# Pairing two lone token tiles across batches, and a re-sorted instruction order, in a fused attention and Fourier mixing kernel

## The chip, the cores and the metric

The kernel runs on one core of a Trainium2 chip. Its engines work side by side and meet only through semaphores: TensorE (PE, with PEld for the loading of weights), VectorE (DVE), ScalarE (ACT), GpSimd (POOL) and SyncE (SP, which only issues DMAs here). The metric is the device time of one execution in microseconds; lower is better.

## The reference

Cosine attention over 8 batches, 12 heads, 448 tokens and 64 features per head, then a Fourier mix and a two-layer network with a residual:

```python
q_n = q / (norm(q) + 1e-06); k_n = k / (norm(k) + 1e-06)
attn = softmax(q_n @ k_n.T / tau)                  # tau = 0.1
x = (attn @ v).transpose(0, 2, 1, 3).reshape(8, 448, 768)
u = x + real(fft(fft(x, axis=1), axis=2))
un = (u - mean(u)) / sqrt(var(u) + 1e-06)
out = u + relu(un @ w_ch1) @ w_ch2                 # 768 -> 3072 -> 768
```

## The kernel before

Python code records every operation of all batches, and a scheduler, the function schedule of class Plan, then lays them out on the five engines. It keeps a clock for each engine, takes durations from a table (TIMES) and times of transfers from another (FLOW), and gives a free engine the ready operation of the lowest priority number. The priority is that of the stage (10 + 100 b for the attention of batch b, 5000 + b for the products of the network, which so fill whatever PE time is left) plus a correction from the table SHIFT, by the operation's name and its count. Only the order goes into the program; each engine then works through its list, and an instruction waits on semaphores for what it reads. So the order of the list is what the scheduler decides, and what a late transfer costs is decided on the chip. The table LATE adds a margin, in microseconds, behind a transfer or a POOL operation on which an operation depends: the scheduler plans its user that much later.

A batch goes through these steps. norm(b) loads q and k, sums squares, scales them (POOL, L896) and transposes them by DMA (SP, L902). attn(b) goes through six pairs of heads. It forms scores by key tile (L973; the last 64 keys by L986), ACT takes the exponential (L951), and PE multiplies by v (L1004, L1010). The scores of one step are written as a group: before the change batches 4 to 7 score three key tiles in a group, batches 1 to 3 two, in groups that run across two head pairs. fft(b) does the Fourier sums on PE (L1134, L1138 over tokens; L1188 and L1191, the last transform, over features, named fd). DVE adds and subtracts them (L1222) and adds them to x (L1233, giving the tiles U and their sums), then normalises each tile to F (L1282, named un). SP transposes it into one of four columns of UNT (L1303, named tru).

A batch has 448 tokens, but works on token tiles of 128: since the transform pairs token t with 448 - t, an even batch has three tiles, and an odd batch four, two of them half filled by an even batch. The network runs over units of one or two such tiles. An up product (L1350) multiplies 128 columns of w_ch1 with a unit: 144 matmuls of 128 columns for a lone tile, 144 of 256 columns for a pair. For a pair the down product (L1494) uses seven products of 12 matmuls (names m1 to m7) instead of eight, with sums of hidden rows formed on DVE (L1593, named s1 to s4) and sums of weights formed once (TX). A lone tile takes four products of 12 (y0 to y3). Some results go through ACT (L1514) and a POOL addition (L1519), the others straight from PSUM on DVE (L1530). Two output tiles, OUTB, collect the result; one kind of tile is stored by SP, the others are scattered by POOL (L1552). The pair of batch 6 and both pairs of batch 7 also save up products in that way (function ups, L1445).

The function units says which tiles go together. Before the change a unit lies within a batch:

```python
for n in (1, 2) if b in (0, self.nb - 2) else (2, 2) if b % 2 else (2, 1):
    sl += [2 * (u % 2) + x for x in range(n)]
```

So batches 0, 2, 4 and 6 have one lone tile each: the first of 0 and 6, the third of 2 and 4. ffn(b) runs the units of batch b, and all products of the network stand in one chain on PE. Where the finished plan leaves a gap on PE in a stretch of little PE work, the function fill puts warm matmuls there (L1737 on W1b), which compute nothing that is used.

Of the kernel before, what the change touches and what calls it, by code (L numbers as in the profile page):

```python
# [13 lines left out]
DM = H * DH  # L14
# [11 lines left out]
TF = 4  # L26
ORDER = (0, 1, 2, 3, 5, 4)
# [456 lines left out]
def t_dve(n, mode=1):  # L484
    return 0.1 + n / (960.0 * mode)
# [15 lines left out]
class Kern:  # L501
# [405 lines left out]
    def attn(self, b):  # L907
# [31 lines left out]
        for pos, j in enumerate(ORDER):  # L939
# [18 lines left out]
            if b < 1:  # L958
                steps = [[(pos, kt)] for kt in range(3)]
            elif b >= 4:  # L960
                steps = [[(pos, kt) for kt in range(3)]]
            else:
                steps = [[(pos, 0), (pos, 1)], [(pos, 2), (pos + 1, 0)]] if pos % 2 == 0 else [[(pos, 1), (pos, 2)]]
# [834 lines left out]
```

## Time and profile before

| | |
|---|---|
| runs | 577.16 us median of 3 (577.0 to 578.32) |
| profiled execution | span 575.2 us from the first to the last instruction; the median of the runs is 1.96 us longer |
| PE busy | 555.8 us, 97% of the span |
| DVE, ACT, POOL busy | 430.6, 385.3, 220.3 us |
| granted TensorE clock | 0.999 of full speed |

Busy times of PE are modelled: a matmul counts from its issue to its end, and successive ones overlap. How fast PE works through a list is read better from the chain of waits, where a piece ends when the next begins. Rows of the trace give start and length in microseconds, engine, line, operation and tiles, and in brackets the idle time before, with what ended it.

### The profile page before, as it was taken

To read this page: it belongs to the slowest core of one execution; us is meant where nothing else is said; L and a number is where in the kernel's file an instruction comes from. 1 tells how busy PE (TensorE), PEld (TensorE's weight loads), DVE (VectorE), ACT (ScalarE), POOL (GpSimd) and SP (SyncE) were. 2 spreads that over 40 slices of the span, in tenths; PEclk is the share of its full clock that TensorE was granted. 3 is DMA by queue.
4 is the path that set the end of the run, shared out by engine and by line. 5 is a ranking of instruction groups with operands and counts; after the bars stand their busy time and mean duration, and the time that the engine had idled before them with its cause. 6 is when DMAs were issued, how large, how long until landed. Compare 5 with 4: busy or idle time off the path is not lost.

```text
span 575.2 us, 16313 instructions
## 1 busy us (share of the span) xinstructions
PE 555.8 (97%) x6766; PEld 436.2 (76%) x6766; DVE 430.6 (75%) x917; ACT 385.3 (67%) x724; POOL 220.3 (38%) x332
## 2 busy tenths in 40 slices
PE   3899999999999999999999999999999999989997
PEld 3569787676787686878788787778778787959694
DVE  8989968996669869975669669776778579986262
ACT  7898885564876885687558875577637853747270
POOL 7534414356329544612370724523270210041303
PEclk9999999999999999999999999999999999999999
DMA  9999999975459739952595429743591210023001
GB/s 188 224 233 171 166 186 130 171 152 111 111 94 103 178 76 135 142 127 62 112 121 93 102 80 147 150 84 85 89 113 29 43 57 28 2 43 72 28 28 56
DMA packets 187898, 62.20 MB, mean 108 GB/s; under 512 B 166800, under 2 KB 185616, under 8 KB 187824
## 3 DMA queue, kind: packets, MB, share of 16 engines
q1 hardware_dynamic: 129856, 38.35, 33.7%
q0 software_dynamic: 57968, 22.81, 30.9%
q8 instruction: 53, 0.87, 0.6%
q14 instruction: 21, 0.17, 0.1%
HBM read 51.90 MB, written 11.01 MB: 109 GB/s over the span
## 4 chain that ended last, share of the span: by engine, by line
PE 60%; DVE 4%; ACT 2%; issue 0%; DVEq 0%; ACTq 0%
PE PS L1494 23%; PE PS L1350 20%; PE PS L1445 6%; PE PS L1010 4%; PE PS L973 3%; DVE U L1233 1%; PE PS L1004 1%; PE PS L986 1%; ACT E L951 1%; DVE ACG L1222 1%; ACT F L1275 1%; PE PS L1134 1%; PE PS L1191 1%; DVE SM L885 1%; DVE HQ L1593 1%
## 5 line engine op out<-in xcount | busy, mean ns | idle before, releaser
L1350 PE MATMUL PS<-UNT,W1b 128*128 128x256 bf16 (+1 forms) x1872 | 186.1, 256 | 1.2 <-DMA UNT<-F 0.6
L1350 PEld LDWEIGHTS PS<-UNT,W1b 128*128 128x128 bf16 x1872 | 155.5, 98 | 20.1 <-issue 2.7
L951 ACT ACTIVATE E<-PS 128x900 bf16<-128x900 f32 (+1 forms) x192 | 148.0, 827 | 19.1 <-PE PS L973 16.6
L1494 PE MATMUL PS<-W2b,HQ 128*128 128x384 bf16 x768 | 133.1, 326 | 0.0
L896 POOL TENSOR_TENSOR QH<-STG,SM 128x256 bf16<-128x256 f32 x126 | 82.3, 679 | 91.9 <-DVE SM L702 73.3
L1494 PEld LDWEIGHTS PS<-W2b,HQ 128*128 128x128 bf16 x768 | 73.3, 98 | 46.2 <-issue 0.7
L1519 POOL TENSOR_TENSOR OUTB<-OUTB,U 128x192 f32<-128x192 f32 x66 | 43.2, 675 | 138.5 <-ACT OUTB L1514 137.3
L1366 ACT ACTIVATE HQ<-PS 128x512 bf16<-128x512 f32 x81 | 48.2, 595 | 40.0 <-PE PS L1350 39.5
L1494 PE MATMUL PS<-TX,HQ 128*128 128x384 bf16 (+2 forms) x408 | 69.7, 321 | 1.8 <-ACT MV L1278 1.6
L883 ACT ACTIVATE QH<-STG 128x384 f32<-128x384 f32 x84 | 42.7, 520 | 25.8 <-DVE SM L885 21.3
L1494 PEld LDWEIGHTS PS<-TX,HQ 128*128 128x128 bf16 x408 | 38.4, 98 | 25.7 <-ACT MV L1278 2.0
L1593 DVE TENSOR_TENSOR HQ<-HQ 128x1536 bf16<-128x1536 bf16 (+1 forms) x69 | 49.5, 721 | 9.9 <-ACT HQ L1366 7.1
L885 DVE TENSOR_REDUCE SM<-QH 128x6 f32<-128x384 f32 x84 | 44.7, 544 | 11.3 <-ACT QH L883 11.0
L1010 PE MATMUL PS<-VB,E 128*128 128x65 bf16 x1152 | 51.4, 193 | 0.0
L1366 DVE TENSOR_SCALAR HQ<-PS 128x512 bf16<-128x512 f32 x45 | 31.0, 688 | 23.8 <-PE PS L1350 23.4
L1010 PEld LDWEIGHTS PS<-VB,E 128*128 128x128 bf16 x1152 | 47.7, 97 | 1.2
L1552 POOL DMA_INDIRECT out_dram<-OUTB,IDX x21 | 23.8, 1134 | 56.9 <-DVE OUTB L1530 51.7
L1004 PE MATMUL PS<-VZ,E 128*128 128x130 bf16 x192 | 41.6, 219 | 0.5 <-ACT E L951 0.2
L973 PE MATMUL PS<-QK 64*128 64x225 bf16 (+2 forms) x864 | 39.6, 227 | 0.1
L1233 DVE SCALAR_TENSOR_TENSOR U<-ACG,X 128x768 bf16<-128x768 f32 (+4 forms) x39 | 39.1, 1015 | 0.8
L1530 DVE TENSOR_TENSOR OUTB<-PS,OUTB 128x384 f32<-128x384 f32 x33 | 18.2, 553 | 25.7 <-PE PS L1494 21.9
L1514 ACT ACTIVATE OUTB<-PS 128x384 f32<-128x384 f32 x33 | 16.1, 488 | 29.5 <-PE PS L1494 29.1
(191 smaller groups left out, 793.6 us busy)
## 6 DMA issues: line engine op xcount, KB each, us to landing
STG<-in_q_dram SPq DMA_DIRECT2D x18, 384.0 KB, 4.0
STG<-in_k_dram SPq DMA_DIRECT2D x18, 384.0 KB, 3.8
VB<-in_v_dram POOLq DMA_DIRECT2D x24, 192.0 KB, 7.1
W1b<-in_moe_w_ch_dram POOLq DMA_DIRECT2D x12, 384.0 KB, 7.7
W2b<-in_moe_w_ch_dram POOLq DMA_DIRECT2D x12, 384.0 KB, 7.2
out_dram<-OUTB SPq DMA_DIRECT2D x7, 384.0 KB, 3.4
W2b<-in_q_dram SPq DMA_DIRECT2D x2, 576.0 KB, 10.0
W2b<-in_k_dram SPq DMA_DIRECT2D x2, 576.0 KB, 10.7
```

The lines of the kernel that those rows point to most:

```text
L885: P.add("dve", lambda v, o=SS[:, i, H // ns * x:H // ns * (x + 1)], sq=sq: v.tensor_reduce(o, sq.rearrange("p (h d) -> p h d", d=DH), AX.X ...
L896: r = v.tensor_tensor(v3(qh)[:, h:h + 4], v3(buf)[:, h:h + 4], RN[:, i, h:h + 4].unsqueeze(2).to_broadcast((128, 4, DH)), AluOp.mult)
L951: return a.activation(o, self.PS[:, bk:bk + nc_, 0:SQ2], ACTF.Exp, scale=1.0 / self.tau)
L973: i = pe.matmul(self.PS[:, bk + h, c0:c0 + n], self.KT[r, jj, kt * 128:(kt + 1) * 128], self.QT[r, jj, cols], start=True, stop=True)
L1004: r = pe.matmul(o, st(6), self.VZ[:, j, :], start=not split, stop=(split and i == 0), skip_group_check=True)
L1010: r = pe.matmul(o[:, 65 * h:65 * h + 65], st(2 * kt + h), self.VB[:, kt, 2 * j + h, :], start=(split and i == h == kt == 0), stop=((not sp ...
L1233: self.snu.append(P.add("dve", lambda v: v.scalar_tensor_tensor(two(U[o0:o0 + n, ut, :]), src, 1.0, two(X[i0:i0 + n, x, :]), AluOp.mult, A ...
L1350: r = pe.matmul(self.PS[:, bk, x * n:(x + 1) * n], self.W1b[:, j, ft * 128:(ft + 1) * 128], self.UNT[:, j, cs], start=(j == 0), stop=(j == ...
L1366: return e.activation(o, i, ACTF.Relu) if e is self.nc.scalar else e.tensor_relu(o, i)
L1494: r = pe.matmul(self.PS[:, bk, 0:n], lhs(f), rhs(f), start=(start and f == 0), stop=(stop and f == NF // 2 - 1), skip_group_check=True)
L1519: r = g.tensor_tensor(self.OUTB[:, ob, xs], self.OUTB[:, ob, xs], self.U[:, ut, xs], AluOp.add)
L1593: P.add("dve", lambda v: v.tensor_tensor(cs(o), cs(a), cs(bq), op), 0.16 + 0.3 * len(ks), -0.5, f"{nm}{ks[0]}_{b}", reads=rd, writes=[x fo ...
```

## The change

Units now run on across batches: all tiles of all batches stand in one list, and two neighbours make a pair except the first tile of batch 0 and the third of batch 2. The third tile of batch 4 is paired with the first of batch 5, and the fourth of batch 5 with the first of batch 6; that tile of batch 5 is normalised later, by the new function unheld, into a buffer of the q and k tiles (QH). A unit runs in ffn of its last batch. Batch 3 scores three key tiles per group, as batches 4 to 7 do, so with 12 matmuls in six groups instead of 8 in nine. The first scores of a batch are ordered behind the last transform of the batch before. LATE is larger for the squares, the copy of key tails (ktd) and of a query column (qdup), and SHIFT has new entries for nearly every operation from batch 1 on. Line numbers grow with the table; L1350 becomes L1714, L1494 L1858, L973 L1317, L1233 L1577, L1282 L1629, L1593 L1958.

```diff
+ONES = ((0, 0), (2, 2))
+HELD = (5, 3)
...
-LATE = {r"W[12]_\d+": 1.5, "tmd": 2.0, r"sq\d_\d": 1.5, r"sq[KQT]\d_1": 1.5, r"ktd\d": 2.0, r"qdup\d": 2.0, r"qk\d._[2-7]": 1.5, ...
+LATE = {r"sq6_[2-7]": 4.0, r"W[12]_\d+": 1.5, "tmd": 2.0, r"sq\d_\d": 2.0, r"sq[KQT]\d_1": 1.5, r"ktd\d": 3.5, r"qdup\d": 4.0, r"qk\d._[2-7]": 1.5, ...
...
+    "fd0_1": {0: -141.9791}, "qe0_1": {0: -36.7192}, "pq0_1": {0: -257.8814, 1: 714.6408}, "u0_1": {0: -254.5074, 1: 210.4266},
...
-            elif b >= 4:
+            elif b >= 3:
                 steps = [[(pos, kt) for kt in range(3)]]
...
-                      tiles=new, acquire=new, margin=0.3, order=([self.last_qk] if self.last_qk else []) + self.pvs[-2:-1])
+                      tiles=new, acquire=new, margin=0.3, order=([self.last_qk] if self.last_qk else []) + self.pvs[-2:-1] + (self.fd_ops[-1:] if b and pos == 0 else []))
...
+            if (b, ui) == HELD:
+                self.held = (ut, rn, lp, slot, col)
+                continue
...
+    def unheld(self):
+        P = self.P
+        ut, rn, lp, slot, col = self.held
+        b, ui = HELD
+        r = self.qh_next % 6
+        self.qh_next += 1
+        qn = [f"QH{r}"] + ["QH1x"] * (r == 1) + ["QH4x"] * (r in (3, 4))
+        P.add("dve", lambda v: v.tensor_scalar(self.QH[:, r, :], self.U[:, ut, 0:DM], self.MV[:, ut, 0:1], self.RS[:, ut:ut + 1], AluOp.add, AluOp.mult),
+              t_dve(DM, 4) + 0.16, lp, f"un{ui}_{b}", reads=rn + [f"MV{ut}", f"RS{ut}"], writes=qn)
+        self.last_tru = P.add("sp", lambda sy, sem: sy.dma_start_transpose(self.UNT[:, :, col:col + 128], self.QH[:, r, :]).then_inc(sem, 16),
...
     def units(self):
+        self.slots = [[0] * len(self.tiles(b)) for b in range(self.nb)]
+        order = [(b, i) for b in range(self.nb) for i in range(len(self.tiles(b)))]
+        u = x = 0
+        self.pairs = []
+        while x < len(order):
+            n = 1 if order[x] in ONES else 2
+            for y in range(n):
+                b, i = order[x + y]
+                self.slots[b][i] = 2 * (u % 2) + y
+            self.pairs.append(order[x:x + n])
+            u, x = u + 1, x + n
...
-        for i, two in ((0, 0), (1, 1)) if b == self.nb - 2 else [(i, i + 1 < len(tiles)) for i in range(0, len(tiles), 2)]:
+        for k, unit in enumerate([u for u in self.pairs if u[-1][0] == b]):
+            two = len(unit) == 2
...
-                    self.up(b, (i, i + 1), chunks, True)
+                    self.up(b, unit, chunks, True)
+                    if unit[1][0] == HELD[0] and unit[0][0] < b:
+                        self.unheld()
```

What the new order does is seen at three joins, on one or two engines each.

PE behind the last transform of batch 5 (L1188, L1191), before the change. The lone tile of batch 4 follows the last down products of the pair before it:

```order
L1188 MATMUL PS<-CS,E 128x96
L1191 MATMUL PS<-CS,E 128x2x96
L1494 MATMUL PS<-W2b,HQ 128x384 x20
L1494 MATMUL PS<-TX,HQ 128x384 x12
L1350 MATMUL PS<-UNT,W1b 128x128 x72
L973 MATMUL PS<-QK 128x128 x2
```

The same place in the change (L1532, L1535 are the transform, L1317 the scores of batch 6):

```order
L1532 MATMUL PS<-CS,E 128x96
L1535 MATMUL PS<-CS,E 128x2x96
L1858 MATMUL PS<-W2b,HQ 128x384 x16
L1858 MATMUL PS<-TX,HQ 128x384 x24
L1858 MATMUL PS<-W2b,HQ 128x384 x16
L1317 MATMUL PS<-QK 128x128 x2
```

Behind it come that group of 24 scores, 12 more down matmuls with the four matmuls of the key tail among them, a second group of 24, and then the joined unit of batches 4 and 5 (L1714, 256 columns). The up product that stood 32 down matmuls behind the transform now stands 76 and two groups behind it.

DVE between the second half of that transform and the first normalised tile, before the change (L1233 adds to U, L1270 the mean, L1282 normalises; L1366 and L885 are evacuations and sums of squares):

```order
L1233 SCALAR_TENSOR_TENSOR U,ACG<-ACG,X 32x768
L1366 TENSOR_SCALAR HQ<-PS 128x512
L1233 SCALAR_TENSOR_TENSOR U,MV<-ACG,X 1x768
L1270 TENSOR_SCALAR MV<-ACG 128x1
L1270 TENSOR_SCALAR MV<-MV 128x1
L885 TENSOR_REDUCE SM<-QH 128x6 x2
L1366 TENSOR_SCALAR HQ<-PS 128x512
L885 TENSOR_REDUCE SM<-QH 128x6
L1366 TENSOR_SCALAR HQ<-PS 128x512
L1282 TENSOR_SCALAR F<-U,MV 128x768
```

And in the change (L1566 subtracts and adds the halves, L1895 adds a product into OUTB, L1577 adds to U, L1629 normalises):

```order
L1566 TENSOR_TENSOR ACG<-PS,ACG 128x388 x2
L1895 TENSOR_TENSOR OUTB<-PS,OUTB 128x384
L1577 SCALAR_TENSOR_TENSOR U,ACG<-ACG,X 97x768
L1629 TENSOR_SCALAR F<-U,MV 128x768
L1229 TENSOR_REDUCE SM<-QH 128x6
L1577 SCALAR_TENSOR_TENSOR U,MV<-ACG,X 64x768
```

The first tile of batch 5 is normalised behind the first addition of the second half, no longer behind all four and their means.

PE in front of the first unit of batch 2, before the change (L973 and L986 are the first scores of batch 3, L1004 and L1010 its products with v; three more such pairs follow, and then L1350 with the unit):

```order
L1494 MATMUL PS<-TX,HQ 128x384 x24
L1494 MATMUL PS<-W2b,HQ 128x384 x8
L973 MATMUL PS<-QK 128x225 x8
L1494 MATMUL PS<-W2b,HQ 128x384 x16
L973 MATMUL PS<-QK 128x225 x8
L1494 MATMUL PS<-TX,HQ 128x384 x4
L986 MATMUL PS<-QK,KTD 128x225 x2
L1494 MATMUL PS<-TX,HQ 128x384 x8
L1004 MATMUL PS<-VZ,E 128x130
L1010 MATMUL PS<-VB,E 128x65 x6
```

And in the change, where L2107 are the warm matmuls:

```order
L1858 MATMUL PS<-TX,HQ 128x384 x24
L1858 MATMUL PS<-W2b,HQ 128x384 x24
L1858 MATMUL PS<-TX,HQ 128x384 x12
L1317 MATMUL PS<-QK 128x225 x12
L2107 MATMUL PS<-W1b 128x128 x18
L1330 MATMUL PS<-QK,KTD 128x225 x2
L1714 MATMUL PS<-UNT,W1b 128x256 x18
```

The products with v that stood in front of the unit are behind it, and 18 warm matmuls have come in.

DVE at the end of batch 6, before the change (L1593 is a comb pass of the network, the second of the two with 1536 columns being s2; L1253 copies, L1465 keeps hidden rows):

```order
L1222 TENSOR_TENSOR ACG<-PS,ACG 128x388 x2
L1593 TENSOR_TENSOR HQ<-HQ 128x512
L1465 TENSOR_TENSOR HQ<-PS,E 128x384
L1233 SCALAR_TENSOR_TENSOR U,ACG<-ACG,X 97x768
L1593 TENSOR_TENSOR HQ<-HQ 128x512
L1253 COPY ACG<-ACG 1x2
L1253 COPY U<-U 1x768
L1593 TENSOR_TENSOR HQ<-HQ 128x1536
L1270 TENSOR_SCALAR MV<-ACG 128x1
L1593 TENSOR_TENSOR HQ<-HQ 128x1536
```

And in the change:

```order
L1566 TENSOR_TENSOR ACG<-PS,ACG 128x388
L1829 TENSOR_TENSOR HQ<-PS,E 128x384 x2
L1831 TENSOR_SCALAR HQ<-HQ 128x384
L1958 TENSOR_TENSOR HQ<-HQ 128x512 x2
L1958 TENSOR_TENSOR HQ<-HQ 128x1536
L1629 TENSOR_SCALAR F<-U,MV 128x768
L1958 TENSOR_TENSOR HQ<-HQ 128x1536
L1566 TENSOR_TENSOR ACG<-PS,ACG 128x388
L1577 SCALAR_TENSOR_TENSOR U,ACG<-ACG,X 97x768
```

One of the two sums, the addition to U and its copies have moved behind the pass s2, and one normalisation ahead of it.

More of the change, by code (lines that the diff above doesn't have):

```diff
@@ L1337, in up @@
         P = self.P
-        sl = [self.slots[b][i] for i in idx]
+        sl = [self.slots[x][i] for x, i in idx]
         n = 128 * len(sl)
@@ L1531, in fin @@
         on = f"OUT{ob}" + "b" * c + "z" * (c0 > 0)
-        return self.P.add("dve", fn, t_dve(c1 - c0), -1, f"{nm}_{b}", reads=([on] if src == "out" else self.unames(b, ut)) + [f"RS{ut}"] * late, writes=[on],
+        return self.P.add("dve", fn, t_dve(c1 - c0), -1, f"{nm}_{b}", reads=([on] if src == "out" else self.unames(bt, ut)) + [f"RS{ut}"] * late, writes=[on],
                           after=(op,), tiles=(tile,))
@@ L1562, in ffn @@
         if b == 0:
-            self.up(0, (0,), range(0, NF, 4), False)
-            self.up(0, (1, 2), range(0, NF, 2), True)
+            self.up(0, ((0, 0),), range(0, NF, 4), False)
+            self.up(0, ((0, 1), (0, 2)), range(0, NF, 2), True)
             for i, ut in enumerate(tiles):
@@ L1600, in ffn @@
                                                                                               channel_multiplier=step), 0.16, -2, f"iz{c}{x}", writes=["IDX", "IDX2"])
-        for i, two in ((0, 0), (1, 1)) if b == self.nb - 2 else [(i, i + 1 < len(tiles)) for i in range(0, len(tiles), 2)]:
+        for k, unit in enumerate([u for u in self.pairs if u[-1][0] == b]):
+            two = len(unit) == 2
+            i = k if b == self.nb - 2 else 2 * k
+            lone = last_b and k == 1
+            b0, u0 = unit[0][0], self.tiles(unit[0][0])[unit[0][1]]
             if two:
-                u0, u1 = tiles[i], tiles[i + 1]
-                if b >= self.nb - 2:
+                u1 = self.tiles(b)[unit[1][1]]
+                if b == self.nb - 1 or unit[0] == (self.nb - 2, 1):
                     if not last_b:
                         self.wsum3()
-                    self.ups(b, (i, i + 1))
+                    self.ups(b, (unit[0][1], unit[1][1]))
                 else:
-                    self.up(b, (i, i + 1), chunks, True)
-                for k in range(3):
-                    comb(4, 2, 3, [k], AluOp.add, "s1")
+                    self.up(b, unit, chunks, True)
+                    if unit[1][0] == HELD[0] and unit[0][0] < b:
+                        self.unheld()
+                for y in range(3):
+                    comb(4, 2, 3, [y], AluOp.add, "s1")
                 comb(2, 2, 0, range(3), AluOp.subtract, "s3")
@@ L1649, in ffn @@
                 continue
-            u0 = tiles[i]
-            self.up(b, (i,), (0, 12, 4, 16, 8, 20), False)
+            self.up(b, unit, (0, 12, 4, 16, 8, 20), False)
             comb(4, 0, 2, range(3), AluOp.add, "s5")
```

39 lines of the change are left out of this document (17 added, 22 removed), and 447 rows, old and new, of the table SHIFT.

## Prediction

> **What bounds the kernel now.** I read the page first: which engine is busy over the whole span, and whether TensorE's clock holds.
>
> ```profile
> PE 555.8 (97%) x6766; PEld 436.2 (76%) x6766; DVE 430.6 (75%) x917; ACT 385.3 (67%) x724; POOL 220.3 (38%) x332
> ...
> PE   3899999999999999999999999999999999989997
> ...
> PEclk9999999999999999999999999999999999999999
> ```
>
> PE is busy in every slice but the first, and the granted clock is full throughout. Next came the busy times by stretch, to see where the idle time lies.
>
> ```profile
> 0.00:75.00 75.00, 61.81 (x889) 50.10 (x890) 67.76 (x161) 64.54 (x113) 38.35 (x72) 1.00 1.31 195
> 75.00:495.00 420.00, 418.94 (x5013) 327.12 (x5011) 316.38 (x664) 282.56 (x536) 162.64 (x228) 1.00 0.63 105
> 495.00:510.00 15.00, 13.36 (x150) 10.14 (x147) 14.24 (x31) 9.33 (x23) 2.43 (x3) 1.00 0.01 2
> 510.00:575.20 65.20, 61.70 (x723) 48.85 (x720) 32.19 (x64) 28.84 (x53) 16.92 (x30) 0.99 0.20 50
> ```
>
> The first number behind the length is PE. Idle are 13.2 us in the first 75, 1.06 us in the 420 that follow, 1.64 us in one place at 504 us. From 75 us on the time is PE's instruction list, and removed matmuls come off the end of the span, if nothing new makes PE wait. DVE has 104 us free in those 420. The chain of waits gives the pace of that list; its columns are start, length, what, and its pieces end where the next begins, so latency is not counted twice.
>
> ```profile
> 213.01 1.31 PE PS L1350 x12
> 214.32 0.49 PE PS L973 x8
> 214.81 1.42 PE PS L1350 x12
> ...
> 301.38 9.17 PE PS L1350 x84
> ...
> 372.86 0.71 PE PS L973 x24
> ...
> 471.27 5.70 PE PS L1350 x102
> ...
> 530.30 13.65 PE PS L1494 x84
> ```
>
> A matmul over a pair (256 columns) takes 9.17/84 = 109.2 ns, over a lone tile (128 columns) 5.70/102 = 55.9 ns, a down matmul (384 columns) 13.65/84 = 162.5 ns. Twelve matmuls behind a group of scores take 1.42 us, elsewhere 1.31: 0.11 us are lost in leaving the group. In its 0.49 us, four pairs of 225 columns at the 0.42 ns a column of the down matmuls account for 0.38: some 0.1 is lost in entering it. A group costs 0.2 us beyond its columns.
>
> **The change, part by part.** *Down products.* The lone tiles of batches 4 and 6 need 2 x 48 matmuls, a pair 7 products x 12 = 84: 12 fewer, 12 x 162.5 ns = **-1.95 us**, all on PE's list.
>
> *Up products.* 288 matmuls of 128 columns become 144 of 256.
>
> ```profile
> L1350 PE MATMUL PS<-UNT,W1b 128*128 128x256 bf16 x1296 | 152.0, 273 | 0.9 <-DMA UNT<-F 0.6 <-DVE QK L799 0.3
> L1350 PE MATMUL PS<-UNT,W1b 128*128 128x128 bf16 x576 | 34.1, 219 | 0.2
> L1350 PEld LDWEIGHTS PS<-UNT,W1b 128*128 128x128 bf16 x1872 | 155.5, 98 | 20.1 <-issue 2.7 <-DVE QK L799 0.4 <-DVE HQ L1366 0.3
> ```
>
> At the pace of the chain that is 16.1 against 15.7 us: -0.4. With small waits counted in, 34.1/576 = 59.2 ns, it is 17.05 against 15.7: -1.3. I take **-0.4**, since the waits inside lone tiles are PE waiting for evacuations, which a pair has too. [...]
>
> *Scores of batch 3.* Nine groups of 8 score matmuls become six of 12, over the same columns: 3 x 0.2 = **-0.6 us** (between -0.3, if groups would have followed each other anyway, and -0.7).
>
> *Passes off PE.* The pair adds six comb passes and drops two, adds three ACT copies and three POOL additions.
>
> ```profile
> L1519 POOL TENSOR_TENSOR OUTB<-OUTB,U 128x192 f32<-128x192 f32 x66 | 43.2, 675 | 138.5 <-ACT OUTB L1514 137.3
> ...
> L1593 DVE TENSOR_TENSOR HQ<-HQ 128x1536 bf16<-128x1536 bf16 (+1 forms) x69 | 49.5, 721 | 9.9 <-ACT HQ L1366 7.1
> ...
> L1530 DVE TENSOR_TENSOR OUTB<-PS,OUTB 128x384 f32<-128x384 f32 x33 | 18.2, 553 | 25.7 <-PE PS L1494 21.9
> ```
>
> Some 4 x 0.72 = 2.9 us of DVE, 6 x 0.68 = 4.1 us of POOL: hidden behind PE (104 and 257 us free in the stretch to 495), 0 on the path. Without that cover they would stand before the products that read them. One scatter of batch 4 (POOL) moves behind batch 5's joined unit, and so ahead of the V loads of batch 7; these wait for batch 6's attention in any case: 0. The transpose of the held tile, on SP, reads a Q/K buffer instead of F; two units of PE work stand before its use: 0.
>
> *The new join.* The unit of batch 4's third tile now needs batch 5's first tile, so PE can wait where it did not. Before, after the transform of batch 5 (ends at 363.2):
>
> ```profile
> 363.22 3.42 PE L1494 MATMUL PS<-W2b,HQ 128*128 128x384 bf16 x20
> 366.47 2.11 PE L1494 MATMUL PS<-TX,HQ 128*128 128x384 bf16 x12
> 368.42 3.77 PE L1350 MATMUL PS<-UNT,W1b 128*128 128x128 bf16 x60
> ```
>
> DVE in the same stretch, from the first addition to U of the transform's second half to the first normalisation:
>
> ```profile
> 370.33 0.94 DVE L1233 SCALAR_TENSOR_TENSOR U<-ACG,X 97x768 bf16<-97x768 f32 x1
> ...
> 378.53 0.48 DVE L1282 TENSOR_SCALAR F<-U,MV 128x768 bf16<-128x768 bf16 x1
> ```
>
> The four transposes into UNT on SP, and the row of their line with the time to landing:
>
> ```profile
> 379.10 5.21 SPq L1303 DMA_TRANSPOSE UNT<-F  x4
> ...
> DMA to landing us min/median/max: 2.7/2.8/5.3
> ```
>
> The lone tile started 5.2 us after the transform, and batch 5's first tile landed at 379.1 + 2.8 = 381.9, 18.7 us after it. In the new order PE has 76 down matmuls (12.35 us), two groups of 24 scores (0.71 + 0.11 each) and a tail (some 0.2) between the transform and the joined unit: 14.2 us of cover. Had DVE kept its order, PE would wait 4.5 us. But DVE's normalisation (L1282, now L1629) stood 8.2 us behind the first addition of the second half (370.33 to 378.53), and now stands directly behind it. Ahead of it DVE has one addition into OUTB that waits for the product m7, 52 down matmuls (8.45 us) after the transform; with that addition 0.55, U 0.94, normalising 0.48 and landing 2.8 the tile is there 13.2 us after the transform. Forecast **0**, with 1.0 us to spare; bounds -0.25 and +4.5. The second join (5 with 6) has 21 products, 13.65 us, and a batch's scores ahead of it, some 20 us: 0.
>
> *Joins of batches 1 and 2, re-sorted.*
>
> ```profile
> 117.90 4.31 PE L1350 MATMUL PS<-UNT,W1b 128*128 128x256 bf16 x38 [0.62 <-DMA UNT<-F]
> ```
>
> ```profile
> 182.11 4.07 PE L1494 MATMUL PS<-TX,HQ 128*128 128x384 bf16 x24
> ...
> 192.08 0.37 PE L986 MATMUL PS<-QK,KTD 128*128 128x225 bf16 x2 [0.15 <-ACT E L951]
> ...
> 194.85 1.38 PE L1350 MATMUL PS<-UNT,W1b 128*128 128x256 bf16 x11
> ```
>
> At 117.9 PE waits 0.62 us for the second tile; its DVE chain now has an OUTB addition and a reduction less ahead of the mean: **-0.4** (0 to -0.6). Batch 2's up starts 12.75 us after its transform (182.1 to 194.85), of which 12.2 are work. Now 68 down matmuls (11.05), one group of 12 scores with its tail (1.0) stand there, 12.05 us, and 18 warm matmuls that compute nothing, 18 x 55.9 ns = 1.0 us. They cover the lag and a little more: a loss of 1.0 in place of 0.5, **+0.5** (0 to +1.5).
>
> *The end of batch 6.* This is the one large wait:
>
> ```profile
> 500.62 4.06 PE L1494 MATMUL PS<-W2b,HQ 128*128 128x384 bf16 x24
> 506.32 4.06 PE L1494 MATMUL PS<-TX,HQ 128*128 128x384 bf16 x24 [1.64 <-ACT MV L1278]
> ...
> 516.07 4.13 PE L1445 MATMUL PS<-UNT,W1b 128*128 128x128 bf16 x71
> ```
>
> ```profile
> 499.96 1.02 DVE L1222 TENSOR_TENSOR ACG<-PS,ACG 128x388 f32<-128x388 f32 x2
> ...
> 501.70 0.95 DVE L1233 SCALAR_TENSOR_TENSOR U<-ACG,X 97x768 bf16<-97x768 f32 x1
> ...
> 503.10 0.34 DVE L1253 COPY U<-U 1x768 bf16<-1x768 bf16 x1
> ...
> 505.22 0.96 DVE L1593 TENSOR_TENSOR HQ<-HQ 128x1536 bf16<-128x1536 bf16 x1 [0.39 <-DVE MV L1270]
> ```
>
> The releaser named is ACT, but the product m6 needs the comb pass s2, which ends at 506.18 on DVE, 0.14 before PE resumes. In the new order an addition to U (0.95), its copies (0.4) and one sum (L1222, 0.5) stand behind s2, and one normalisation (0.48) has moved ahead: about 1.4 us earlier. **-1.2** (0 to -1.6). What is late next is batch 7's first tile, used at 516.07; its passes move some 2 us back, about the slack that they have.
>
> *Fresh waits.* A whole re-sorted list has waits that no row of before shows. The old one lost 1.06 us between 75 and 495; I put as much again, **+1.1**, with ends 0 (a list as tight) and +4.5 (one join missed as priced above).
>
> Sum: -1.95 - 0.4 - 0.6 - 0.4 + 0.5 - 1.2 + 1.1 = **-2.95 us**. The profiled span is 575.2, the median of the runs 577.16: 1.96 us lie around the span, which the change does not touch. Span 572.2, time 574.2 us.
>
> **Rivals.** *The gain is eaten.* 2.95 us of PE work go, but waits of 1.3 to 4.5 us appear and the end keeps its 1.64. For it: single waits of 0.15 to 0.62 us in the old list, each of which a new order can put at more places; larger margins put the users of transfers later, and something must fill that time. Against: the same scheduler left 1.06 us idle in 420. Time about 577 us.
>
> *The joined unit waits* (slower). Place: PE before batch 4 and 5's unit. If tile (5,0) lands later than 14.2 us after the transform, PE stands, and everything behind it. From 18.9 us the wait (4.7) exceeds the 2.95 by 1.73 us, and the kernel is slower. For it: 18.7 us in before, and the OUTB addition ahead of the normalisation ties it to m7. Against: the new place of the normalisation. A landing at 21 us gives 6.8 - 2.95: 581 us. [...]
>
> *Lone tiles bound by weight loads.* If a 128-column matmul cost its load, 98 ns in the LDWEIGHTS row, pairing would save 288 x 98 ns - 15.7 = 12.5 us: 564 us. The chain's 55.9 ns speak against it. [...]
>
> **How the numbers follow.** No change within the measurement's reach is 0.3%, 1.73 us: 575.4 to 578.9. Chances: forecast 0.62, eaten 0.25, joined unit waits 0.11, weight loads 0.02. Faster 0.64, same 0.25, slower 0.11. The range: below, the sum without fresh waits and with the upper saving of the up products, -2.95 - 1.1 - 0.9 - 0.4 = -5.35, 571.8, and 0.4 more for the wait at 506 gone whole: 571.4; above, into the eaten case until 1 in 8 is left out, 578.4.
>
> **What would show it.** Right: PE busy falls by some 3 us; the 128-column up matmuls outside batches 0 and 2 are gone (288 left); the down matmuls fall by 12; the wait at 504 is under 0.6 us; no wait above 0.5 us before the joined units. Wrong: a PE wait on DMA into UNT before the first joined unit, PE idle above 2.5 us between 75 and 495, or an unbroken wait before the products of batch 7.

## The result: slower, and the profile after

| | before | changed |
|---|---|---|
| median of 9 runs each | 578.34 us (577.0 to 579.44) | 582.16 us (579.97 to 582.84) |
| ratio, with its 95% interval | | 1.0054 (1.0043 to 1.0065) |
| profiled execution: span, time | 575.2, 577.16 us | 578.2, 580.05 us |

The forecast was 574.2 us; the change costs 3 to 4 us. (The quotient of the two medians is 1.0066; the ratio of the table, with its interval, is the one used below.) The busy times by stretch of the changed kernel, PE first behind the length:

```profile
0.00:75.00 75.00, 61.05 (x881) 49.52 (x882) 67.11 (x159) 65.02 (x114) 38.38 (x73) 1.00 1.34 196
75.00:495.00 420.00, 413.83 (x4799) 320.49 (x4798) 318.59 (x661) 278.50 (x533) 169.62 (x234) 1.00 0.67 105
495.00:510.00 15.00, 15.00 (x215) 13.16 (x213) 13.84 (x33) 10.04 (x23) 1.72 (x2) 1.00 0.06 12
510.00:578.20 68.20, 64.75 (x741) 50.37 (x738) 36.75 (x72) 31.10 (x59) 16.68 (x30) 1.00 0.17 45
```

PE's idle time goes from 1.06 to 6.17 us between 75 and 495, from 1.64 to 0 at the end of batch 6, from 13.19 to 13.95 in the first 75 us and from 3.50 to 3.45 behind 510. That is 4.2 us more idle, against 1.2 us less busy. The first stretch is scatter: PE's first up product stood between 48.0 and 50.2 us in the traces of all kernels here. The first line of the page:

```profile
PE 554.6 (96%) x6628; PEld 433.6 (75%) x6628; DVE 436.3 (75%) x922; ACT 384.7 (67%) x726; POOL 226.4 (39%) x338
```

138 matmuls fewer are 144 up and 12 down matmuls less, and 18 warm ones more (1.0 us): by these two traces some 2.2 us of PE work are gone, and between 75 and 495 us 5.1 us of new waits came. Here they are in PE's timeline, each row being the work that resumes, with its wait in brackets:

```profile
192.42 0.82 PE L1858 MATMUL PS<-TX,HQ 128*128 128x384 bf16 x4 [2.04 <-DVE OUTB L1895]
...
228.61 1.47 PE L1858 MATMUL PS<-TX,HQ 128*128 128x384 bf16 x8 [0.33 <-DVE OUTB L1895]
...
236.58 0.60 PE L1482 MATMUL PS<-CS,F 128*97 128x225 bf16 x4 [1.00 <-DVE F L1442]
...
296.91 1.00 PE L1478 MATMUL PS<-CS,F 128*128 128x113 bf16 x16 [0.46 <-DVE F L1442]
...
378.21 1.05 PE L1714 MATMUL PS<-UNT,W1b 128*128 128x256 bf16 x8 [0.34 <-DVE HQ L1730]
...
445.05 0.81 PE L1858 MATMUL PS<-W2b,HQ 128*128 128x384 bf16 x4 [0.75 <-ACT MV L1624]
...
487.41 0.82 PE L1858 MATMUL PS<-TX,HQ 128*128 128x384 bf16 x4 [0.90 <-DVE OUTB L1895]
```

They sum to 5.8 of the 6.17 us, and none is at a transfer into UNT. Four stand in the seven products of a pair, where a product continues on a PSUM tile that ACT or DVE must have read first; two before the Fourier sums of batches 3 and 4; one in the joined unit of batches 4 and 5, at an evacuation.

The longest one followed back. PE needs DVE's addition into OUTB (L1895, fin31_1), which needs the second of two POOL additions (fm2p_1 behind fv2p_1). POOL's timeline:

```profile
182.35 6.73 POOL L1240 TENSOR_TENSOR QH<-STG,SM 128x256 bf16<-128x256 f32 x6 [0.79 <-DVE SM L1046]
189.22 1.06 POOL L1884 TENSOR_TENSOR OUTB<-OUTB,U 128x192 f32<-128x192 f32 x2
190.72 1.05 POOL L1884 TENSOR_TENSOR OUTB<-OUTB,U 128x192 f32<-128x192 f32 x2 [0.44 <-ACT MV L1624]
```

POOL was scaling q and k for batch 3 until 189 us, and the two additions came behind that. On POOL's old list they stand behind the same scaling, but there they ended at 189.82 us, 2.0 earlier, and PE did not wait for them. Two waits are a matter of a single row in another queue. ACT before the wait at 445 (L1295 is an exponential of batch 7, L1879 the copy fm2_5 that PE waits for):

```profile
443.63 0.90 ACT L1295 ACTIVATE E<-PS 128x900 bf16<-128x900 f32 x1
444.43 0.47 ACT L1879 ACTIVATE OUTB<-PS 128x384 f32<-128x384 f32 x1
```

The releaser that the row names, L1624, is not the last one: by time it is L1879, which ends at 444.90. And DVE before the wait at 487 (L1751, L1762 form sums of weights for batch 7's units, L1895 is what PE waits for):

```profile
483.36 1.30 DVE L1751 TENSOR_TENSOR QK<-W1b,QH 128x1536 bf16<-128x1536 bf16 x1
484.58 1.10 DVE L1391 TENSOR_TENSOR ACG<-X 128x512 bf16<-128x512 bf16 x2
485.61 0.94 DVE L1762 TENSOR_TENSOR W1b<-W1b 128x1536 bf16<-128x1536 bf16 x1
486.47 0.41 DVE L1398 TENSOR_TENSOR F<-ACG 128x512 bf16<-128x512 bf16 x1
486.81 0.54 DVE L1895 TENSOR_TENSOR OUTB<-PS,OUTB 128x384 f32<-128x384 f32 x1
```

### The profile page after: what moved, and what is told of

Read it like the earlier page. It is cut to its first block, busy times and chain, and to the rows that moved or that the text cites. A ratio compares the mean times of both kernels' runs of the same rounds, so it can differ in the third digit from the quotient of the medians.

```text
span 578.2 us, 16067 instructions
## 1 busy us (share of the span) xinstructions
PE 554.6 (96%) x6628; PEld 433.6 (75%) x6628; DVE 436.3 (75%) x922; ACT 384.7 (67%) x726; POOL 226.4 (39%) x338
## 4 chain that ended last, share of the span: by engine, by line
PE 71%; DVE 18%; ACT 4%; POOL 3%; issue 3%; POOLq 0%; DVEq 0%; ACTq 0%
PE PS L1714 25%; PE PS L1858 22%; PE PS L1809 7%; PE PS L1354 5%; PE PS L1317 5%; DVE U L1577 2%; PE PS L1348 2%; DVE HQ L1958 2%; ACT E L1295 1%; DVE OUTB L1895 1%; PE PS L1330 1%; DVE TX L2047 1%; POOL QH L1240 1%; POOL OUTB L1884 1%; DVE ACG L1391 1%
## 5 line engine op out<-in xcount | busy, mean ns | idle before, releaser
L1714 PE MATMUL PS<-UNT,W1b 128*128 128x256 bf16 (+1 forms) x1728 | 185.3, 264 | 1.2 <-DVE TX L1730 0.4
L1295 ACT ACTIVATE E<-PS 128x900 bf16<-128x900 f32 (+1 forms) x192 | 149.7, 826 | 29.1 <-PE PS L1317 23.8
L1714 PEld LDWEIGHTS PS<-UNT,W1b 128*128 128x128 bf16 x1728 | 153.3, 98 | 20.9 <-issue 1.9
L1240 POOL TENSOR_TENSOR QH<-STG,SM 128x256 bf16<-128x256 f32 x126 | 86.0, 709 | 111.2 <-DVE SM L1046 81.9
L1858 PE MATMUL PS<-W2b,HQ 128*128 128x384 bf16 x720 | 125.1, 326 | 0.7 <-ACT MV L1624 0.7
L1858 PEld LDWEIGHTS PS<-W2b,HQ 128*128 128x128 bf16 x720 | 68.7, 98 | 44.2 <-DVE U L1577 1.1
L1884 POOL TENSOR_TENSOR OUTB<-OUTB,U 128x192 f32<-128x192 f32 x72 | 48.4, 692 | 111.3 <-ACT OUTB L1879 109.3
L1858 PE MATMUL PS<-TX,HQ 128*128 128x384 bf16 (+2 forms) x444 | 76.4, 322 | 3.3 <-DVE OUTB L1895 3.3
L1858 PEld LDWEIGHTS PS<-TX,HQ 128*128 128x128 bf16 x444 | 41.4, 98 | 30.3 <-DVE OUTB L1895 5.3
L1958 DVE TENSOR_TENSOR HQ<-HQ 128x1536 bf16<-128x1536 bf16 (+1 forms) x73 | 52.0, 715 | 9.9 <-ACT HQ L1730 5.6
L1730 DVE TENSOR_SCALAR HQ<-PS 128x512 bf16<-128x512 f32 x42 | 28.9, 689 | 21.5 <-PE PS L1714 21.2
L1879 ACT ACTIVATE OUTB<-PS 128x384 f32<-128x384 f32 x36 | 17.7, 491 | 38.9 <-PE PS L1858 38.9
L1577 DVE SCALAR_TENSOR_TENSOR U<-ACG,X 128x768 bf16<-128x768 f32 (+4 forms) x39 | 38.6, 998 | 0.8
L1317 PE MATMUL PS<-QK 64*128 64x225 bf16 (+2 forms) x864 | 39.2, 227 | 0.1
L1619 ACT ACTIVATE F<-U,MV 128x768 bf16<-128x768 bf16 x28 | 26.0, 930 | 18.3 <-DVE MV L1614 13.1
```

What stands on the lines that cost most here:

```text
L1240: r = v.tensor_tensor(v3(qh)[:, h:h + 4], v3(buf)[:, h:h + 4], RN[:, i, h:h + 4].unsqueeze(2).to_broadcast((128, 4, DH)), AluOp.mult)
L1295: return a.activation(o, self.PS[:, bk:bk + nc_, 0:SQ2], ACTF.Exp, scale=1.0 / self.tau)
L1317: i = pe.matmul(self.PS[:, bk + h, c0:c0 + n], self.KT[r, jj, kt * 128:(kt + 1) * 128], self.QT[r, jj, cols], start=True, stop=True)
L1577: self.snu.append(P.add("dve", lambda v: v.scalar_tensor_tensor(two(U[o0:o0 + n, ut, :]), src, 1.0, two(X[i0:i0 + n, x, :]), AluOp.mult, A ...
L1714: r = pe.matmul(self.PS[:, bk, x * n:(x + 1) * n], self.W1b[:, j, ft * 128:(ft + 1) * 128], self.UNT[:, j, cs], start=(j == 0), stop=(j == ...
L1730: return e.activation(o, i, ACTF.Relu) if e is self.nc.scalar else e.tensor_relu(o, i)
```

## The experiments

All kernels but the one with the old entries change only the finished lists, behind the scheduler: an operation is taken out of its engine's list and put behind another one, or matmuls that compute nothing used are added or taken out. In each line of `moves` stand the engine, the operation and its count, and the operation, with its count, behind which it is put. Every ratio is to the kernel before, measured in the same session; the kernel with the old entries was run once only.

```diff
+        moves = (
+            ('dve', 'rcp3', 3, 'eps3', 3),
+            ('pool', 'fm2p_1', 0, 'sc5_3', 0),
+        )
+        for e in self.P.ENGS:
...
+            for m in todo:
+                L.insert(L.index(key[m[3], m[4]]) + 1, key[m[1], m[2]])
         self.P.emit(self.nc, self.es)
```

**Do the new waits eat the gain?** *Two moves*, those above.

> The changed kernel with two operations moved in its lists: on POOL the second addition into OUTB of batch 1's last pair (fm2p_1) ahead of the first one (fv2p_1), and on DVE the reciprocal of batch 3's norms (rcp3) one place ahead. Nothing is added or left out. Theory O (the new order eats the gain: each wait of PE that it brings in is lost once and comes off the end when it is removed): in the changed kernel PE stands 2.2 us before the last product of that pair, since the addition that it reads is second of two on POOL (1.05 us each, with 0.4 between) behind 6.7 us of scaling passes. With it first the wait shrinks by about 1.4 us, and the span by as much: ratio to the kernel before about 1.003 (1.0022 to 1.0040) where the changed kernel has 1.0054. Theory S (DVE and POOL are the bound between 180 and 300 us, so that a wait taken away returns at the next join, before the Fourier sums of batch 3 or 4): ratio 1.0050 to 1.0058.

Measured 1.0000 (0.9988 to 1.0012), below the range of either theory. POOL and PE in this kernel:

```profile
182.79 5.67 POOL L1240 TENSOR_TENSOR QH<-STG,SM 128x256 bf16<-128x256 f32 x6 [0.51 <-DVE SM L1046]
188.61 2.91 POOL L1884 TENSOR_TENSOR OUTB<-OUTB,U 128x192 f32<-128x192 f32 x4
```

```profile
187.05 4.06 PE L1858 MATMUL PS<-W2b,HQ 128*128 128x384 bf16 x24
191.13 2.12 PE L1858 MATMUL PS<-TX,HQ 128*128 128x384 bf16 x12
...
194.36 1.19 PE L2107 MATMUL PS<-W1b 128*128 128x128 bf16 x18 [0.42 <-DVE OUTB L1895]
```

The wait of 2.04 us is gone (191.13 - 187.05 = 4.08 us for 24 matmuls, 0.2 more than their pace). Some 0.8 us of it came back right behind, as two short waits that the changed kernel does not have: 0.42 in the last row, 0.39 at 198.4. At the Fourier sums, where S expected it, the waits are as they were (1.05 and 0.52 us). That a wait taken away only comes back elsewhere (S) does not hold for this one. But the gain of 0.0054 is 3.1 us, with an uncertainty of 0.9, more than the wait: something else hung on it, see below.

*Eleven moves*, on the other waits:

```diff
+            ('act', 'ex1_3', 0, 'nrm4', 0), ('act', 'relu18_3', 0, 'nrm5', 2), ('act', 'fm2_5', 0, 'ln21_6', 0),
+            ('act', 'k21_6', 0, 'c1r1_6', 0), ('act', 'fv1_6', 0, 'fa1_6', 0), ('dve', 't30', 0, 'fin21_0', 0),
+            ('dve', 'ktd5', 0, 'fin11_3', 0), ('dve', 'te1_4', 0, 'ss6_5', 1), ('dve', 'S32', 0, 'g1_7', 1),
+            ('dve', 'c11_6', 0, 'hb0_7', 0), ('dve', 'fin10_6', 1, 'pq1_7', 1),
```

> The changed kernel with eleven other operations moved in ACT's and DVE's lists, most by one place: ACT's copy fm2_5 ahead of the exponential behind which it stood at 444 us, an exponential of batch 3 and an evacuation of batch 3 one place ahead (200 and 275 us), two copies of batch 6 one place ahead; on DVE a copy of key tails (ktd5) and a sum of weights (S32) six places back, behind the folding of batch 4 and 7's attention that the Fourier sums and the product at 486 us wait for, and four more by one place. By the durations of the changed kernel's trace, theory O expects about 3.0 us less, from waits at 200, 278, 296, 444, 486 and 505 us: ratio about 1.000 (0.9990 to 1.0015). Theory S expects that only the waits at 444 and 486, where DVE and ACT have time to spare, come off, at most 1 us: 1.0035 or more.

Measured 1.0011 (1.0002 to 1.0021): 2.5 us off, as O has it. *Thirteen moves*, both sets:

> Both sets of moves together, in the changed kernel. Theory O: the two gains add, 4.4 us: ratio about 0.998 (0.9965 to 0.9990), so faster than the kernel before by what the prediction had for the change itself, and single waits of over 0.5 us left at 236 us only. Theory S: 1.003 or more. A third theory, W, has the 3.0 us in the work itself (a pair across batches, the second addition and its passes, or the warm matmuls cost more than counted): then the moves give little, and PE's busy time, not its idle time, is what exceeds the forecast.

> The kernel with the thirteen moves once more, as the kernel that the next two are held against, on their chip: ratio 0.9970 to 0.9990.

Measured 0.9980 (0.9968 to 0.9991) and again 0.9980 (0.9972 to 0.9989), median 576.91 us beside 578.18: the changed kernel with 13 operations moved beats both kernels. No matmul was added or taken out for it: the order alone does it, against W. Added, the two gains would have made 0.9957; the shortfall of 0.0023 is about as large as its uncertainty. One wait of over 0.5 us is left that O did not expect, 0.7 us at 517 (shown further below).

**What else hung on the longest wait?** *Without the warm matmuls* at 195 us, first:

```diff
+        self.P.order["pe"] = [op for op in self.P.order["pe"] if op.name != "warm" or op.start < 150.0]
```

> The changed kernel without the three groups of six warm matmuls at 195 us; they compute nothing that is used. If they cost PE time, as the prediction had it (1.0 us of work in place of a wait of 0.5): 0.5 to 1.1 us less, ratio 1.0035 to 1.0046. If they only fill a wait (the four matmuls of the key tail behind them need an exponential that ACT ends at 196.4 us in the changed kernel): the same time, 1.0050 to 1.0058, and an idle stretch of about 1.2 us in their place, without a lower granted clock behind it.

Measured 1.0046 (1.0025 to 1.0068), which by itself decides little. Its trace shows a second thing, PE behind the same wait:

```profile
188.82 1.79 PE L1858 MATMUL PS<-W2b,HQ 128*128 128x384 bf16 x10
192.65 3.58 PE L1858 MATMUL PS<-TX,HQ 128*128 128x384 bf16 x12 [2.04 <-DVE OUTB L1895]
196.16 0.93 PE L1317 MATMUL PS<-QK 64*128 64x225 bf16 x12
198.11 0.37 PE L1330 MATMUL PS<-QK,KTD 128*128 128x225 bf16 x2 [1.02 <-ACT E L1295]
```

Twelve matmuls take 3.58 us behind the wait, ten took 1.79 ahead of it. And the 18 warm matmuls had stood in a wait for an exponential: without them PE idles 1.02 us in their place, so they cost nothing there. The next two test the clock.

> The changed kernel as it is, on the same chip as the next three. Theory G: the wait of 2.2 us at 190 us costs more than itself, because in most executions the granted clock falls to a half behind it for some 3.4 us (in the trace of the kernel without the warm matmuls it was 1.00 up to 193 us, 0.57, 0.50, 0.50 and 0.72 in the next four us, and 11 down matmuls took 3.41 us where the changed kernel's profiled execution has 10 in 1.79). That execution had kept its clock and took 580.05 us, the median was 582.16. So the ratio is again 1.0045 to 1.0065, more than half of the executions have a mean clock of 0.997 or less, and these are 1 to 2 us longer than the others. Without G: the clock is as in the kernel before (three of 28 executions at 0.997) and the ratio is 1.003 to 1.005.

Measured 1.0058 (1.0046 to 1.0071); in five of six executions the mean clock was 0.997 or less (582.4 to 583.7 us), in one 0.999 (581.2). In the first nine runs it was six, median 582.4, against 580.05, 580.6 and 581.0 us for the other three; but one of the six, at 579.97, was the shortest of all. The stretches around the wait in the trace of this second run (583.65 us, mean clock 0.997); the granted clock is the third number from the end:

```profile
190.00:192.00 2.00, 0.95 (x6) 0.36 (x4) 0.00 (x0) 0.91 (x4) 1.56 (x4) 1.00 1.34 235
192.00:193.00 1.00, 0.02 (x1) 0.03 (x2) 0.60 (x2) 0.00 (x0) 0.33 (x1) 1.00 0.70 157
193.00:194.00 1.00, 1.00 (x7) 0.61 (x8) 0.97 (x3) 0.00 (x0) 0.00 (x0) 1.00 1.23 272
194.00:195.00 1.00, 1.00 (x5) 0.52 (x4) 1.00 (x4) 0.48 (x1) 0.00 (x0) 0.55 1.27 199
195.00:196.00 1.00, 1.00 (x5) 0.28 (x5) 0.41 (x1) 1.00 (x4) 0.77 (x1) 0.50 0.48 96
196.00:197.00 1.00, 1.00 (x12) 0.61 (x10) 0.95 (x3) 0.15 (x1) 0.31 (x1) 0.50 0.99 213
197.00:198.00 1.00, 1.00 (x16) 0.88 (x14) 0.94 (x3) 0.77 (x1) 0.86 (x1) 0.74 0.79 320
```

One microsecond after PE resumes its clock falls to a half, for some 3.4 us, which costs half of that, 1.7. The first profiled execution had the same wait and kept its clock. The counts fit: with the wait kept, the mean clock was 0.997 or less in 8 of 12 executions (eleven moves) and 6 of 7 (without the warm matmuls), with it taken away in 1 of 12 (two moves).

*Warm matmuls in the wait*, 36 of them ahead of the product that waits:

```diff
+        at = [i for i, op in enumerate(L) if op.name == "m42_1"][0]
...
+        for x in range(6):
...
+            L.insert(at, op)
```

> The changed kernel with six more groups of six warm matmuls (36 x 55.9 ns, 2.0 us), which compute nothing that is used, on PE in the wait at 190 us, ahead of the product m4 that waits there. The wait for the addition stays as it is. Theory G: the array stays busy, the clock does not fall, nine in ten executions have a mean clock of 0.999 or more, and the ratio comes down by about 1.5 us to 1.0025 to 1.0040. If the clock has another cause, or its fall costs nothing: ratio and clocks as in the changed kernel, 1.0045 to 1.0065.

Measured 1.0031 (1.0019 to 1.0043), all executions 580.65 to 581.28 us:

```profile
187.82 3.09 PE L1858 MATMUL PS<-W2b,HQ 128*128 128x384 bf16 x18
190.75 2.17 PE L2107 MATMUL PS<-W1b 128*128 128x128 bf16 x36
192.88 1.31 PE L1858 MATMUL PS<-TX,HQ 128*128 128x384 bf16 x7
```

The product still waits as long, yet 0.0027, 1.6 us, came off, close to the 1.7 us of the trace: that is the price of the clock. Taking the wait away too gives the other 0.0031, 1.8 us, of two_moves; each of the two shares is uncertain by about 1 us. One part of the expectation missed: two of six executions still had 0.997. The trace of one of them has its clock low between 14 and 18 us (0.57 and 0.58 in two stretches of 2 us), in the start, and at 1.00 here; so a mean of 0.997 does not say where the clock was low.

**How much more is in the order?** *25 and 31 further moves*, some on PE, and without the warm matmuls:

```diff
+            ('pe', 'h16_6', 0, 'pv31_7', 0), ('dve', 'ss6_5', 0, 'e1_4', 0), ('dve', 'fin11_6', 0, 'fa1_7', 1), ...
```

> The kernel with the thirteen moves, 25 further moves by one to three places (8 of them before 190 us, six on PE), and without the warm matmuls at 195 us. Theory O: the waits that the thirteen left at 194 (0.3), 296 (0.5), 455 (0.3), 484 (0.4) and 516 us (0.85) come off in part, 2.4 us by the durations of its trace; waits at 197, 226 and 234 us stay. Ratio 0.994 (0.9925 to 0.9965). Theory S: no better than the thirteen moves, 0.9975 or more.

> Another set of 31 moves on top of the thirteen, by up to nine places, again without the warm matmuls at 195 us; it should take the wait at 226 us as well. Theory O: 2.8 us less than the thirteen moves, ratio 0.993 (0.9915 to 0.9965); less sure than the other set, since operations stand further from where the trace has timed them beside others. Theory S: 0.9975 or more.

Measured 1.0018 (0.9998 to 1.0038) and 0.9991 (0.9975 to 1.0008): both expectations of O missed. In 8 and 7 of 12 executions the mean clock was 0.997 or less, and the longest (up to 584.2 us) are among these; with the thirteen moves, which keep the warm matmuls, it was 2 of 9 and 0 of 11. That those warm matmuls, between two waits, keep the clock up is not shown: these kernels also have moves on PE, and the one trace of such an execution (31 moves) has its clock low between 14 and 18 us (0.59 and 0.56), in the start, and at 1.00 from 190 to 200. With 24 matmuls added at the Fourier sums, below, it is 5 of 12 though the warm ones stay.

*22 and 30 further moves* on DVE and ACT alone, warm matmuls kept:

```diff
+            ('dve', 'ss6_5', 0, 'fin11_3', 0), ('act', 'te0_4', 0, 'sq6_5', 1), ('dve', 'un0_5', 0, 'fin11_4', 0), ...
```

> The kernel with the thirteen moves and 22 more, on DVE and ACT alone (mostly by one or two places; PE's list stays as the scheduler made it, and the warm matmuls at 195 us stay). Theory O: the two sets tried before lost what they won, since their moves on PE put matmuls ahead of waits that the older traces did not show (1.4 us at 276, 1.7 at 300 in one, 1.4 to 1.8 at four places between 460 and 520 in the other); without them the waits at 296, 484 and 516 us come off, 2.1 us: ratio 0.9945 (0.9930 to 0.9970). If the waits only hop: 0.9970 or more.

> As the kernel before it, with another set of 30 moves on DVE and ACT on top of the thirteen; it should also take the wait at 226 us and the one at 361 us, where a sum of squares that waits for a late load stands ahead of a pass that PE needs. Theory O: 2.8 us less than the thirteen moves, 0.993 (0.9915 to 0.9965). If the waits only hop: 0.9970 or more.

Measured 0.9981 (0.9970 to 0.9992) and 0.9980 (0.9968 to 0.9993), no better than the thirteen moves. The reason that the first of these expectations gives was misread: what it calls waits at 276, 300 and 460 to 520 us is largely the work of the PE operations moved there, whose rows follow each other; only the one at 519 us, for a transfer into UNT, is a wait (2.18 us, with 25 moves). The clock is low in 0 and 1 of 12 executions. So beyond the thirteen moves the waits do come back elsewhere, as S had it: 1.15 us at 363 with 22 moves (0.33 at most with the thirteen alone) and 0.81 at 142 with 30. (Both traces are of long executions, 578.64 and 579.27 us.) O, by which the order is at fault, holds up to the thirteen. PE in the kernel with 30 moves, the batch 3 sums and batch 7's first products:

```profile
237.35 0.57 PE L1482 MATMUL PS<-CS,F 128*97 128x225 bf16 x4 [1.31 <-DVE F L1442]
...
518.96 1.24 PE L1809 MATMUL PS<-UNT,W1b 128*128 128x128 bf16 x19 [0.90 <-DMA UNT<-F]
```

*18 moves in the kernel before*, two of which put s3 and s2 of batch 6 ahead:

```diff
+            ('dve', 's30_6', 0, 's12_6', 0), ('dve', 's20_6', 0, 's30_6', 0), ('act', 'ex0_4', 0, 'sq1_5', 1), ...
```

> The kernel before the change, its units and tables unchanged, with 18 operations moved by one or two places on DVE and ACT, found in its own trace in the same way. Two of them put the passes s3 and s2 of batch 6 one and two places ahead, and so take the wait of 1.64 us at 504 us, which the prediction counted as the change's gain. By the durations of its trace 2.0 us less: ratio 0.9965 (0.9950 to 0.9985). Theory O with the counted work: the changed structure is then worth what the prediction gave its matmuls, 2 to 3 us, between the best order of the one and of the other. If the old order has no such reserve: 0.9990 to 1.0010.

Measured 0.9989 (0.9980 to 0.9998), about half of the gain expected. Its largest wait, 1.64 us before, is now:

```profile
506.53 2.12 PE L1494 MATMUL PS<-TX,HQ 128*128 128x384 bf16 x12 [0.58 <-DVE HQ L1593]
```

A second one of 0.33 us follows it, so that PE idles 0.91 us of that stretch instead of 1.64. The changed structure in the best order tried is then 0.0009 ahead of the old one, with an uncertainty of some 0.0014: not the 2 to 3 us expected.

*The old entries* with the changed structure:

> The changed structure (pairs across batches, three key tiles per group in batch 3, the held tile) with the tables SHIFT and LATE of the kernel before. The entries were made for another list of operations; the scheduler's own plan ends at 651 us with them, against 566 for the changed kernel and 568 for the kernel before, and has 232 groups of warm matmuls in its gaps. If the plan is a fair picture: 655 to 670 us. If the order hardly matters and the structure carries the change: 575 to 585 us.

One execution: 664.07 us. The structure cannot be tried without a table made for it; with the table of the other list it takes 82 us more.

**Do removed matmuls come off the end at all?** 24 matmuls added to the kernel with the thirteen moves, at two places without a wait (the first line), and at two waits (the second):

```diff
+        for ref, bank, last in (('m22_5', 2, 'pq0_6'), ('m20_6', 2, 'x5_7')):
...
+        for ref, bank, last in (('fs0_3', 2, 'x4_3'), ('fs0_4', 6, 'x4_4')):
```

> The kernel with the thirteen moves, and 24 matmuls of 384 columns put into PE's list, twice as many as the change took out, in two groups of 12: ahead of the second product of batch 5's last unit and of batch 6's first (428 and 475 us), where PE runs without a wait. They compute nothing that is used. If PE's list sets the pace there, so that the 12 removed matmuls came off the end as counted: 24 x 162.5 ns = 3.9 us more, ratio 1.0035 to 1.0060. If DVE or the transfers set it and PE's matmuls lie beside them: 0.9985 to 1.0010 (at most 1 us more).

> The same 24 matmuls in two groups of 12, but directly in front of the Fourier sums of batches 3 and 4 (233 and 294 us), where PE still waits 1.04 and 0.52 us for the folding of the attention on DVE. If these two waits are DVE's own pace, the matmuls fill them and cost 3.9 - 1.56 = 2.3 us: ratio 1.0010 to 1.0035, about 1.6 us less than the kernel before this one. If the waits were only an effect of where PE stood, they come back behind the added work: 1.0035 to 1.0060.

Measured 1.0034 (1.0022 to 1.0045) and 1.0018 (1.0008 to 1.0028), against 0.9980: 3.1 and 2.2 us more, of 3.9. At the waits, the kernel that they are held against and the one with added matmuls (L2141):

```profile
236.04 0.57 PE L1482 MATMUL PS<-CS,F 128*97 128x225 bf16 x4 [1.05 <-DVE F L1442]
...
296.29 0.38 PE L1478 MATMUL PS<-CS,F 128*128 128x113 bf16 x4 [0.36 <-DVE F L1442]
```

```profile
232.57 2.11 PE L2141 MATMUL PS<-W1b 128*128 128x384 bf16 x12
234.53 0.56 PE L1482 MATMUL PS<-CS,F 128*97 128x225 bf16 x4
...
294.52 2.11 PE L2141 MATMUL PS<-W1b 128*128 128x384 bf16 x12
296.47 0.73 PE L1478 MATMUL PS<-CS,F 128*128 128x113 bf16 x11
```

The Fourier sums follow the added matmuls at once, 12 of which take the pace of 1.96 us: these two waits were DVE's own pace, and filling them is free. Elsewhere PE's list is the bound: 3.1 of the 3.9 us reach the end, with an uncertainty of 0.8, so that all of it is not ruled out.

## Why the prediction was wrong, step by step

*Fresh waits, +1.1 us: the step that failed.* Idle time between 75 and 495 us rose by 5.1 us, beyond the upper end of 4.5; the sign named for it, PE idle above 2.5 us there, came with 6.17. The argument was that the same scheduler had left 1.06 us idle. But what is idle on the chip is not what the scheduler planned, which had the changed kernel ahead, at 566 us against 568. It is what its durations got wrong, at places where the result of one engine is used with little to spare; this is argued, from the scaling passes on POOL (see the end), and not tested by itself. A small idle time in one list says how well that list happens to fit, not how well another will. The bracket's upper end priced one late join; seven places were late. The rival "the gain is eaten" named the mechanism, and its waits reached 4.5 us, but its time was put at 577 us, no slower than before. A slower kernel was priced only for a wait at the joined unit. That waits of 0.3 to 2.0 us at many places can together exceed the 2.95 was left out, and none of the rows quoted excluded it.

*A term was missing.* The profile's clock rows stood at full speed, and the sum had no term for a lower clock behind a wait. Here a wait of 2.0 us costs another 1.6 us through the clock (1.0058 against 1.0031 with matmuls in the wait), in most executions. It accounts for most of the 2.1 us by which the median (582.16) lies above the profiled execution, which had kept its clock.

*Down products -1.95, up -0.4, scores -0.6.* Sign and mechanism right: added matmuls of the same kind cost 3.1 us for 3.9 counted, and PE's work fell by some 2.2 us where 2.95 were counted. Whether a term is short is open: two traces of the kernel with the thirteen moves differ by 2.0 us in PE's busy time (555.4 and 557.4).

*Passes off PE, 0: not refuted, but argued from totals.* DVE and POOL did have the time. What PE waited for at 192 us are not the passes that this term prices: those two additions belong to batch 1's last pair, which the old kernel has too. They show what totals miss: an engine at 39% can be late by the order of its queue.

*New joins, 0: right, mechanism and size.* Neither joined unit waited for its tile; the first one's up products started 14.2 us after the transform (360.90 to 375.07), as forecast, and the wait at 378 us is for an evacuation. The rival on the slower side, the joined unit, was the wrong place.

*Batch 1's join, -0.4: right.* The wait of 0.62 us is 0.16 at 118 us in the changed kernel.

*Batch 2's join, +0.5: wrong in size and reason.* The transform of batch 2 ends at 181.12 us in the changed kernel. The row of the warm matmuls, and the first up product:

```profile
195.37 1.19 PE L2107 MATMUL PS<-W1b 128*128 128x128 bf16 x18
196.46 0.37 PE L1330 MATMUL PS<-QK,KTD 128*128 128x225 bf16 x2
196.83 1.36 PE L1714 MATMUL PS<-UNT,W1b 128*128 128x256 bf16 x11
```

That is 15.7 us, where the prediction had 12.05 of work and 1.0 of warm matmuls: the wait of 2.04 us stands in this very join. The term asked only when batch 2's tile lands, and not whether the 68 down matmuls in front of it can run through. The warm matmuls themselves fill a wait for an exponential and cost nothing. (The 2.04 us are part of the 5.1 above, not in addition to them.)

*End of batch 6, -1.2: measured -1.64.* But it was order, not structure: moves in the old lists take 0.73 of the 1.64 us as well. The next thing late there is batch 7's tile, as named; with the thirteen moves, where PE comes earlier, it costs 0.7 us.

Still open is where the 1.3 us went by which the two sets of moves do not add, if they are more than noise. Part of it can be the wait at batch 7's tile in the row below, from the kernel with the thirteen moves; of the two traces of the changed kernel one has none there and one 0.53 us, and that with two moves has none:

```profile
517.87 1.34 PE L1809 MATMUL PS<-UNT,W1b 128*128 128x128 bf16 x21 [0.71 <-DMA UNT<-F]
```

## What to carry to other kernels

When a change re-sorts a list that runs within 1% of its bound, price the new waits by how many results each engine hands over with under 2 us to spare, not by the idle time of the old list (a way of counting that no run here has tested). After such a change read every bracket on the bound engine, follow it back to the one queue in which the needed result stands second, and swap it there: two moved operations gave back 3.1 us, thirteen gave a kernel at 0.998. Here a wait of 2.0 us on TensorE cost 3.1 us, about 1.6 of it through the clock, and matmuls that compute nothing, put into the wait, gave that part back.

## What the runs showed of the hardware

Behind an idle time of 2.0 us in an otherwise busy list, the granted clock fell to 0.50 to 0.57 for about 3.4 us in two traces: the second of the changed kernel, and that of the kernel without the warm matmuls. In the first trace of the changed kernel and that of the eleven moves it stayed at 1.00 behind the same wait. Half of 3.4 us is 0.003 of the span, which is the mean clock of 0.997; 6 of 9 and 5 of 6 executions of the changed kernel had that or less. So 2.0 us were enough in two of four traces, and no run shows what decides between them.

POOL's scaling pass is not of one length: the 126 of the changed kernel took 0.602 to 1.420 us, with a median of 0.613. Two of them, POOL and then DVE:

```profile
182.35 1.20 POOL L1240 TENSOR_TENSOR QH<-STG,SM 128x256 bf16<-128x256 f32 x1 [0.79 <-DVE SM L1046]
...
186.32 0.61 POOL L1240 TENSOR_TENSOR QH<-STG,SM 128x256 bf16<-128x256 f32 x1
```

```profile
182.19 0.89 DVE L1577 SCALAR_TENSOR_TENSOR U<-ACG,X 128x768 bf16<-128x768 f32 x1
...
185.82 1.03 DVE L1566 TENSOR_TENSOR ACG<-PS,ACG 128x388 f32<-128x388 f32 x2
```

It took 1.20 us beside a DVE pass with two inputs from SBUF, and 0.61 beside one that reads PSUM; the three others that fell beside a pass of the first kind took 1.32 to 1.42. In these rows the time of POOL's queue goes with what DVE does at that moment; no run changed DVE's pass alone. The six passes ahead of the longest wait took 6.73 us here, 5.80 in the kernel before and 5.67 with two moves, where six of 0.61 are 3.7.
